# New homes for block 1's transposed activations and for the inner operands of a two-block MLP kernel

## The chip, the core and the metric

The kernel runs on one core of a Trainium2 chip. The metric is the device time of one execution, in microseconds (us), lower is better; the median of three runs stands for a kernel. The core has a matrix engine (TensorE, PE in the profile), a vector engine (VectorE, DVE), an activation engine (ScalarE, ACT), GpSimd (POOL) and SyncE (SP), which here issues nearly all transfers. Each engine works through its own list of instructions in order, and waits at semaphores for the others.

## The reference, cut to what matters

```python
B, S, D, F = 1, 2048, 1024, 3584          # all inputs bfloat16

def reference(x, w1, b1, w2, b2):
    y = _layernorm(x, axis=-1)            # over D, no scale, no shift
    h = _gelu(jnp.einsum("bsd,df->bsf", y, w1) + b1)    # tanh form
    return jnp.einsum("bsf,fd->bsd", h, w2) + b2
```

## The kernel before

The 2048 rows are worked on in two blocks of 1024 (`s` = 0 and 1). Both matrix products of a block use Strassen's scheme in Winograd's form: an operand is cut into quarters (11, 12, 21, 22), sums of quarters (S1 to S4 on one side, T1 to T4 on the other) are made on VectorE, and seven products (numbers 1 to 7) take the place of eight.

- The first product has 7 chunks of w1 per block (`NC` = 7), loaded into a ring of 3 slots. The chunks of both blocks are counted through: 0 to 6 in block 0, 7 to 13 in block 1; chunk `n` lies in slot `n % 3`.
- The second product runs its seven products in the order 5, 1, 2, 6, 7, 3, 4. Products 1 to 4 are cut once more into seven ("inner" products, `INNER`), whose operand sums need room: four X operands in the tile of the T sums of w1 (`t1_sb`), four Y operands of 7 x 256 = 1792 elements in the w1 ring. Inner product 4 has other places for them.
- `yw_sb` is shared. During the first product it holds the transposed activations: A11, A12, A21, A22 and the sums S1 to S4, in seven slots of 2048 elements (A21 and S3 share one). During the second product its quarter "C", the first 7168 elements (3.5 slots), holds the w2 operand of product 2.

Block 1 is prepared while block 0's second product runs: rows are loaded, normalized on ScalarE (`ln_act2`), transposed by DMA into `yw_sb` (`dma_T`), summed on VectorE (`y_sums`), and the first w1 chunks are loaded.

The order of the instructions on each engine isn't written by hand. Every operation is handed to a planner with its dependencies, a modelled cost and a priority; the planner simulates the engines, picks at each moment the most urgent operation among those that could start, and thereby fixes each engine's list. A changed dependency can therefore change the order on several engines.

```python
        YN = KH * HT                                    # 4 * 512 = 2048
        yop = {n: yw16[:, k * YN:(k + 1) * YN].rearrange("p (k n) -> p k n", n=HT)
               for k, n in enumerate(("A11", "A12", "A22", "S3", "S1", "S2", "S4"))}
        yop["A21"] = yop["S3"]
...
        w2q = {"A": w2a_sb[:, 0], "B": w2a_sb[:, 1], "C": quarter(yw_sb, 0), "D": quarter(yw_sb, 1)}
...
        def load_w1(s, c, prio, gate=(), eng="SP"):
            n = s * NC + c
            deps = [*w1_use.get(n - N_W1, ()), *gate]   # N_W1 = 3
            w1_ld[(s, c)] = [dma(w1_sb[:, n % N_W1, ...], ...) for j in range(2)]   # two halves of 512 KB
...
        def dma_T(s, i, prio, gate):                    # tile i of 8: 128 rows; halves k of D
            for k in range(2):
                res.append(add("SP", 1.4, lambda e, k=k: e.dma_start_transpose(
                    dst_y(i, k), x16[:, i, k * HT:(k + 1) * HT]), (y_ok[(s, i)], *gate[k]), ...))
        # dst_y: tiles 0 to 3 go to A11 (k = 0) and A12 (k = 1), tiles 4 to 7 to A21 and A22; TH = 4
...
        def y_sums(s, prio, gate=(), war=()):           # each sum in two instructions
            S1 = tt("S1", "A21", "A22", ALU.add, ())
            S2 = tt("S2", "S1", "A11", ALU.subtract, (S1,))
            S3 = tt("S3", "A11", "A21", ALU.subtract, (S1,))
            S4 = tt("S4", "A12", "S2", ALU.subtract, (S2,))
...
        def mm2_block(s, W):
            ...
            X0 = halves(t1_sb ...)
            Y0 = halves(w1_16 ...)                      # elements 0 to 7167 of the ring's 3 * 4096
            n = s * NC + NC - 1
            ...                                         # products 5, 1, 2, 6, 7
            B[2] = load_w2(s, "C", "B21", W["C"], base2[s])       # W["C"]: all matmuls of the first product
            ...
            sub3 = inner(3, S4, B[3], X0, Y0, ...)
            for m in range(n - 2, n + 1):
                w1_use[m] = w1_use[m] + done(3)         # the slots are released by inner product 3
            ...
            inner(4, A[22], B[4], ...)
            return {"A": done(3), "B": done(4), "C": done(2), "ring": ring, "w1": [(), (), ()]}
...
            if s + 1 < NSB:
                for c in range(N_W1):
                    load_w1(s + 1, c, base2[s] + 40 + c, wf["w1"][c])
                for i in range(NT):                     # 8 tiles
                    load_x(s + 1, i, [*x_gate[i]], base2[s] - 4 + i)
                    ln_act2(s + 1, i, base2[s] + 10 + 5 * i, wf["ring"])
                    dma_T(s + 1, i, base2[s] + 30 + 3 * i, (wf["C"], wf["C"]))
                y_sums(s + 1, base1[s + 1] - 14, wf["C"])
```

`w1_use[m]` are the instructions that read chunk `m`, so that the load into its slot three chunks later waits for them. `done(p)` are the matmuls and operand sums of product `p`. `last` (not in this cut) are the matmuls of the block's first product.

Of the kernel before, what the change touches and what calls it, by code (L numbers as in the profile page):

```python
# [26 lines left out]
N_W1 = 3  # L27
# [57 lines left out]
class Planner:  # L85
# [8 lines left out]
    def add(self, *a, **k):  # L94
        o = Op(*a, **k)
        self.ops.append(o)
        return o
# [139 lines left out]
def bass_standalone__mixer_channel_mlp__prompt_kernel(  # L237
# [19 lines left out]
    TH = HT // P  # L257
# [4 lines left out]
    with ExitStack() as es:  # L262
# [28 lines left out]
        w1_16 = w1_sb[:, :, :, :].bitcast(FP16)  # L291
# [6 lines left out]
        def quarter(t, k):  # L298
# [4 lines left out]
        tq = nc.dram_tensor("w2_sums", [4, P, NU, HT], FP16, kind="Internal").ap()  # L303
        YN = KH * HT
        yop = {n: yw16[:, k * YN:(k + 1) * YN].rearrange("p (k n) -> p k n", n=HT)
               for k, n in enumerate(("A11", "A12", "A22", "S3", "S1", "S2", "S4"))}
        yop["A21"] = yop["S3"]

        pl = Planner()
# [9 lines left out]
        base2 = [b + T_MM1 for b in base1]  # L319


        def dma(dst, src, deps, prio, name, sem, nbytes, eng="SP", late=0.0):
            return add(eng, 0.42 if eng == "SP" else 0.45, lambda e: e.dma_start(dst, src), deps, prio, name,
                       sem="d_" + sem, inc=16, nbytes=nbytes, late=late)
# [16 lines left out]
        def load_w1(s, c, prio, gate=(), eng="SP"):  # L341
            n = s * NC + c
            deps = [*w1_use.get(n - N_W1, ()), *gate]
            w1_ld[(s, c)] = [dma(w1_sb[:, n % N_W1, j * KH:(j + 1) * KH, :],
                                 w1v[:, j * KH:(j + 1) * KH, c * 4 * P:(c + 1) * 4 * P], deps, prio + 0.01 * j,
                                 f"w1_{s}_{c}_{j}", f"w1_{n % N_W1}_{j}", KH * P * 4 * P * 2, eng=eng) for j in range(2)]
# [114 lines left out]
        def dst_y(i, k):  # L461
            return yop[("A1" if i < TH else "A2") + "12"[k]][:, :, (i % TH) * P:(i % TH + 1) * P]
# [18 lines left out]
        def dma_T(s, i, prio, gate):  # L481
            res = []
            for k in range(2):
                res.append(add("SP", 1.4, lambda e, k=k: e.dma_start_transpose(  # L484
                    dst_y(i, k), x16[:, i, k * HT:(k + 1) * HT]), (y_ok[(s, i)], *gate[k]), prio + 0.05 * k,
                    f"yt{s}_{i}_{k}", sem=f"d_yt{i}{k}", inc=16, nbytes=P * HT * 2))
            x_free[(s, i)] = res
            y_in[(s, i)] = res
# [4 lines left out]
        def y_sums(s, prio, gate=(), war=()):  # L493
# [5 lines left out]
            def tt(n, x0, x1, op, dp):  # L499
                res = []  # L500
                deps = [o for x in (x0, x1) for o in src.get(x, ())]
                for g in range(2):
                    sl = slice(g * KP, (g + 1) * KP)
                    res.append(add("DVE", 0.64, lambda e, sl=sl: e.tensor_tensor(  # L504
                        out=yop[n][:, sl, :], in0=yop[x0][:, sl, :], in1=yop[x1][:, sl, :], op=op),
                        [*deps, *gate, *(war if n == "S3" else ())] + [d[g] for d in dp],
                        prio + {"S1": 0, "S2": 1, "S4": 2, "S3": 3}[n] + 0.1 * g, f"y{n}_{s}_{g}"))
                return res
# [5 lines that stand above are left out]
            opnd[s] = {n: [src[n]] * KH for n in ("A11", "A12", "A22")}  # L514
            for n, l in (("S1", S1), ("S2", S2), ("S3", S3), ("S4", S4)):
                opnd[s][n] = [[l[k // KP]] for k in range(KH)]
# [146 lines left out]
        KI = NU // 2  # L663
        HI = HT // 2
# [3 lines left out]
        def sums(dst, a, b, op, deps, prio, name, step=2):  # L668

            res = []  # L670
            n = len(a[1])
            cuts = step if isinstance(step, tuple) else tuple([step] * (n // step) + [n % step] * (n % step > 0))
            k0 = 0
            for g, w in enumerate(cuts):
                k1 = k0 + w
                dl = list(deps)
                for k in range(k0, k1):
                    dl += a[1][k] + b[1][k]
                o = add("DVE", cost2(w * dst.shape[-1]), lambda e, k0=k0, k1=k1: e.tensor_tensor(  # L679
                    out=dst[:, k0:k1, :], in0=a[0][:, k0:k1, :], in1=b[0][:, k0:k1, :], op=op),  # L680
                    list(dict.fromkeys(dl)), prio + 0.15 * k0, f"{name}_{g}")
                res += [[o]] * w
                k0 = k1
            return dst, res
# [4 lines left out]
        def uniq(*a):  # L689
            return list(dict.fromkeys(o for l in a for o in l))  # L690
# [55 lines left out]
        def mm2_block(s, W):  # L746
# [6 lines left out]
            A = {q: (h[q], [[h_ok[(s, q, u)]] for u in range(NU)]) for q in h}  # L753
            users = {p: [] for p in SEQ2}
            done = lambda p: users[p]
# [144 lines left out]
                return subs  # L900

            def halves(t):
                return [t[:, r * KI * HI:(r + 1) * KI * HI].rearrange("p (k n) -> p k n", n=HI) for r in range(4)]

            X0 = halves(t1_sb[:, :, :, :, :].rearrange("p a b k c -> p (a b k c)"))
            Y0 = halves(w1_16[:, :, :, :].rearrange("p a k c -> p (a k c)"))
            n = s * NC + NC - 1
            S1 = sums(h[21], A[21], A[22], ALU.add, (), pt[5] - 12, f"hS1_{s}")
            ring = uniq(*(w1_use[m] for m in range(n - 2, n + 1)), *(l for m in (n - 1, n) for l in t1_use[m].values()))
            war0 = {(c, r): ring + S1[1][-1] for c in "ST" for r in range(1, 8)}  # L910

            def war_of(subs):
                return {(c, r): [subs[r]] for c in "ST" for r in subs}

            B = dict(W)
# [6 lines left out]
            for t in range(TH):  # L922
# [5 lines left out]
            hb = [Holder(banks, seeded=True) for _ in range(TH)]  # L928
            g1, ok1, sub1 = inner(1, A[11], B[1], X0, Y0, war0, gate=(M5[2],), bias=(
                b2_sb[:, None, 0:HI].to_broadcast([P, 2, HI]), e0_sb[:, None, :].to_broadcast([P, 2, HI])))  # L930
# [3 lines left out]
            S2 = sums(h[11], S1, A[11], ALU.subtract, done(1), pt[2], f"hS2_{s}", step=(2, 4, 4, 4))  # L934
            S3 = sums(h[21], A[22], S2, ALU.subtract, done(5), pt[2] + 4, f"hS3_{s}", step=(4, 4, 4, 2))
# [3 lines left out]
            okw = {11: ok1[11], 12: sdb[1], 21: sdb[3], 22: sdb[3]}  # L939
            sub2 = inner(2, A[12], B[2], X0, Y0, war_of(sub1), O=(g1, okw), out=11)  # L940
            S4 = sums(h[12], A[12], S2, ALU.subtract, done(2), pt[6], f"hS4_{s}", step=(4, 4, 4, 2))
# [22 lines left out]
                               alloc=g3 if t == 0 else None, frees=(hb[t],)))  # L964

            sub3 = inner(3, S4, B[3], X0, Y0, war_of(sub2), O=(g12, {11: O12[1], 12: O12[1], 21: O12[3], 22: O12[3]}), out=12)
            for m in range(n - 2, n + 1):
                w1_use[m] = w1_use[m] + done(3)
            for m in (n - 1, n):
                for k in range(1, 5):  # L970
# [8 lines left out]
            hf = {11: done(4), 12: done(3), 21: done(4), 22: done(4) + flat(S3)}  # L979
            for q in h:  # L980
                h_war[(s + 1, q)] = hf[q]
            return {"A": done(3), "B": done(4), "C": done(2), "ring": ring, "w1": [(), (), ()]}

        tile_prio = [-100 + 2.3 * i for i in range(NT)]
        for i in range(NT):
# [19 lines left out]
        for s in range(NSB):  # L1005
            last = []
            for c in range(NC):
                n = s * NC + c
                t0 = base1[s] + c * 14 * SLOT
                if n:  # L1010
                    T = w1_sums(s, c, t0 - 2 * SLOT)
                    for v in range(2):
                        last += mm1_unit(s, c, v, T, t0 + v * SLOT)
                m = n + N_W1
                if m < (s + 1) * NC:
                    load_w1(s, m % NC, t0 + 14 * SLOT)
                if s == 0 and c == 1:
                    gate = (w1_use[0][-1],)
                    t11 = load_w2(0, "B", "B11", gate, t0 + 0.1)
                    t1q = w2_prep(t11[1][0][0], gate, t0 + 8, 8.5)  # L1020
            if s == 0:
                W = {5: t1q, 1: t11}
            else:
                W = {5: load_w2(s, "A", "T1", wfree["A"], base1[s] + 0.3 * T_MM1),
                     1: load_w2(s, "B", "B11", wfree["B"], base1[s] + 0.3 * T_MM1 + 0.1)}
            W["C"] = last
            wfree = wf = mm2_block(s, W)
            if s + 1 < NSB:
                for c in range(N_W1):
                    load_w1(s + 1, c, base2[s] + 40 + c, wf["w1"][c])  # L1030
                for i in range(NT):
                    load_x(s + 1, i, [*x_gate[i]], base2[s] - 4 + i)
                    ln_act2(s + 1, i, base2[s] + 10 + 5 * i, wf["ring"])
                    dma_T(s + 1, i, base2[s] + 30 + 3 * i, (wf["C"], wf["C"]))
                y_sums(s + 1, base1[s + 1] - 14, wf["C"])

        order = pl.place()
# [57 lines left out]
```

## Time and profile before

| what | value |
|---|---|
| time, median of 3 runs | 352.75 us (351.5 to 354.36) |
| span of the profiled run | 351.5 us |
| TensorE busy | 338.8 us, 96% |
| VectorE busy | 255.3 us, 73% |
| ScalarE busy | 183.6 us, 52% |
| DMA, mean of 16 engines | 179 GB/s |
| granted TensorE clock | 1.00 |

"Busy" is an average over the whole span. The stages, by TensorE's timeline: head and first chunk to about 30 us, block 0's first product to 100.2 us, its second product to about 175 us (with some of it up to 188 us), block 1's first product to 268.7 us, its second product to 347.9 us. In the lines of the profile, L604 are the matmuls of the first product, L792 those of the plain products of the second, L838 those of the inner products; L679 are the operand sums of the second product on VectorE, L504 those of the activations, L537 those of w1. `yw_sb<-x_sb` are the transposes, `w_sb<-in_w_dram` the loads of w1 (digits are dropped from names: `w_sb` is `w1_sb`, `t_sb` is `t1_sb`), `w2a_sb` two homes of w2 operands. SPq is the time that SyncE's queue took to issue transfers, not the transfers themselves. A bracket after a line is the idle time of the engine before it and what ended it.

### The profile page before, as it was taken

How to read it: one execution, taken by the hardware profiler on the slowest of the kernel's cores; microseconds unless marked ns; L12 is line 12 of the kernel's file. 1: busy time of each engine (PE TensorE's matmuls, PEld its weight loads, DVE VectorE, ACT ScalarE, POOL GpSimd, SP SyncE). 2: the span in 40 equal slices, each digit the busy share in tenths (PEclk: the TensorE clock that was granted, in tenths of full speed). 3: DMA queues.
4: the chain of work that ended last, by engine and by line, in shares of the span. 5: the costliest groups of instructions: out<-in, count | busy, mean ns of one | idle time of the engine just before them, and what ended most of it. 6: DMA issues, size and time to landing. Idle time of an engine off the chain costs nothing.

```text
span 351.5 us, 5462 instructions
## 1 busy us (share of the span) xinstructions
PE 338.8 (96%) x2179; PEld 202.6 (58%) x2179; DVE 255.3 (73%) x356; ACT 183.6 (52%) x303; POOL 23.5 (7%) x47
## 2 busy tenths in 40 slices
PE   4999999999999999999859999999999999999995
PEld 4987444444445876448735444444444488644885
DVE  5679988988575797969399665375338869896943
ACT  3674766766798888431113766767677234001110
POOL 2320000000004123600000000000000000000000
PEclk9999999999999999999999999999999999999999
DMA  7748999979863450798699730330002355019111
GB/s 233 247 91 279 354 341 342 300 270 300 277 202 85 186 211 21 140 385 129 154 370 339 259 97 24 119 119 2 0 0 87 123 212 210 32 48 400 62 62 60
DMA packets 54339, 63.01 MB, mean 179 GB/s; under 512 B 12970, under 2 KB 47786, under 8 KB 53418
## 3 DMA queue, kind: packets, MB, share of 16 engines
q1 hardware_dynamic: 54170, 62.54, 55.0%
q8 instruction: 17, 0.28, 0.3%
q10 hardware_dynamic: 144, 0.13, 0.1%
q14 instruction: 8, 0.07, 0.1%
HBM read 48.50 MB, written 11.53 MB: 171 GB/s over the span
## 4 chain that ended last, share of the span: by engine, by line
PE 85%; DVE 5%; DMA 4%; SPq 3%; issue 1%; ACT 1%; DVEq 0%
PE ps L604 44%; PE ps L838 20%; PE ps L792 15%; PE ps L562 5%; SPq L484 3%; DMA w2a_sb<-in_w_dram 2%; DVE h_sb L679 2%; DMA x_sb<-in_x_dram 1%; DVE o_sb L756 1%; DVE w_sb L679 1%; PE ps L468 1%; DVE yw_sb L504 1%; DMA yw_sb<-x_sb 1%; DVE sn_sb L756 0%; ACT h_sb L410 0%
## 5 line engine op out<-in xcount | busy, mean ns | idle before, releaser
L604 PE MATMUL ps<-yw_sb,t_sb 128*128 128x512 f16 x416 | 96.2, 379 | 0.0
L604 PE MATMUL ps<-yw_sb,w_sb 128*128 128x512 f16 x312 | 73.7, 379 | 1.8 <-DMA w_sb<-in_w_dram 1.8
L792 PE MATMUL ps<-w2a_sb,h_sb 128*128 128x512 f16 x336 | 73.8, 379 | 0.0
L604 PEld LDWEIGHTS ps<-yw_sb,t_sb 128*128 128x128 f16 x416 | 40.5, 98 | 48.8 <-ACT sn_sb L617 0.6
L622 DVE TENSOR_TENSOR sn_sb<-ps,sn_sb 128x512 f32<-128x512 f32 x54 | 36.6, 689 | 25.9 <-PE ps L604 25.8
L792 PEld LDWEIGHTS ps<-w2a_sb,h_sb 128*128 128x128 f16 x336 | 32.9, 98 | 38.4
L604 PEld LDWEIGHTS ps<-yw_sb,w_sb 128*128 128x128 bf16 x312 | 30.3, 98 | 38.3 <-DMA w_sb<-in_w_dram 2.1
L628 ACT ACTIVATE h_sb<-sn_sb,b_sb 128x512 f16<-128x512 f32 x54 | 38.6, 719 | 18.7 <-DVE sn_sb L622 16.3
L776 ACT COPY sn_sb<-ps 128x512 f32<-128x512 f32 x30 | 17.3, 581 | 46.9 <-DVE o_sb L756 34.8
L617 ACT COPY sn_sb<-ps 128x512 f32<-128x512 f32 x49 | 28.7, 586 | 23.1 <-PE ps L604 22.9
L679 DVE TENSOR_TENSOR h_sb<-h_sb 128x1024 f16<-128x1024 f16 (+2 forms) x42 | 38.6, 951 | 2.1 <-ACT h_sb L628 2.1
L628 ACT ACTIVATE h_sb<-ps,b_sb 128x512 f16<-128x512 f32 x50 | 34.1, 685 | 9.1 <-PE ps L604 8.2
L756 DVE TENSOR_TENSOR o_sb<-ps,sn_sb 128x512 bf16<-128x512 f32 x32 | 21.9, 688 | 13.5 <-PE ps L838 9.5
L838 PE MATMUL ps<-w_sb,t_sb 128*128 128x256 f16 x252 | 30.0, 273 | 0.0
L838 PEld LDWEIGHTS ps<-w_sb,t_sb 128*128 128x128 f16 x252 | 24.7, 98 | 3.1
L537 DVE TENSOR_TENSOR t_sb<-w_sb,t_sb 128x1024 f16<-128x1024 bf16 x26 | 17.9, 688 | 8.3 <-PE ps L604 7.9
L838 PE MATMUL ps<-w2a_sb,h_sb 128*128 128x256 bf16 (+1 forms) x182 | 21.8, 273 | 0.0
L537 DVE TENSOR_TENSOR t_sb<-w_sb 128x1024 f16<-128x1024 bf16 x26 | 17.8, 683 | 5.5 <-PE ps L604 4.1
L776 ACT COPY ps<-sn_sb 128x512 f32<-128x512 f32 x14 | 8.1, 588 | 24.4 <-PE ps L838 20.5
L679 DVE TENSOR_TENSOR t_sb<-h_sb 128x1792 f16<-128x1792 f16 x12 | 13.0, 1086 | 9.6 <-PE ps L838 9.5
L838 PEld LDWEIGHTS ps<-w2a_sb,h_sb 128*128 128x128 f16 x182 | 17.7, 98 | 3.2
L756 DVE TENSOR_TENSOR sn_sb<-ps,sn_sb 128x512 f32<-128x512 f32 x24 | 16.5, 686 | 4.2 <-PE ps L838 2.6
(82 smaller groups left out, 322.0 us busy)
## 6 DMA issues: line engine op xcount, KB each, us to landing
w_sb<-in_w_dram SPq DMA_DIRECT2D x28, 512.0 KB, 5.4
w2a_sb<-w_sums SPq DMA_DIRECT2D x5, 1792.0 KB, 7.5
w2a_sb<-in_w_dram SPq DMA_DIRECT2D x4, 1792.0 KB, 8.6
x_sb<-in_w_dram SPq DMA_DIRECT2D x21, 256.0 KB, 4.8
w_sums<-x_sb SPq DMA_DIRECT2D x21, 256.0 KB, 4.6
x_sb<-in_x_dram SPq DMA_DIRECT2D x15, 256.0 KB, 4.3
yw_sb<-in_w_dram SPq DMA_DIRECT2D x2, 1792.0 KB, 7.6
h_sb<-w_sums SPq DMA_DIRECT2D x2, 1792.0 KB, 11.5
```

The source lines that it names most:

```text
L484: res.append(add("SP", 1.4, lambda e, k=k: e.dma_start_transpose(dst_y(i, k), x16[:, i, k * HT:(k + 1) * HT]), (y_ok[(s, i)], *gate[k]), p ...
L537: return add("DVE", 0.65, lambda e: e.tensor_tensor(out=tv(k), in0=x0, in1=x1, op=ALU.subtract), [*deps, *war.get(k, ())], prio + 0.5 * k, ...
L562: fn = [(lambda e, b=b, hb=hold[f], f=f, k=k, t=t: e.matmul(ps[:, hb.k, t * P:(t + 1) * P], lhsT=lhs[:, k, f * P:(f + 1) * P], rhs=yop[f"A ...
L604: fn = [(lambda e, k=k: e.matmul(ps[:, hold[p].k, :], lhsT=lhs[:, k, :], rhs=yop[yo][:, k, :], start=(first and k == 0), stop=(k == KH - 1 ...
L617: return e.copy(out=dst, in_=src) if o_.eng == "ACT" else e.tensor_copy(dst, src)
L622: return add("DVE", 0.69, lambda e: e.tensor_tensor(out=sn_sb[:, hold_s.k, :], in0=ps[:, hold[p].k, :], in1=sn_sb[:, hold_s.k, :], op=ALU. ...
L628: r = h_ok[(s, q, u)] = add("ACT", 0.70, lambda e: e.activation(out=h[q][:, u, :], in_=src(), func=ACT.Gelu_apprx_tanh, bias=b1_sb[:, f:f ...
L679: o = add("DVE", cost2(w * dst.shape[-1]), lambda e, k0=k0, k1=k1: e.tensor_tensor(out=dst[:, k0:k1, :], in0=a[0][:, k0:k1, :], in1=b[0][: ...
L756: plus = lambda e, out, x, y: e.tensor_tensor(out=out, in0=x, in1=y, op=ALU.add)
L776: return act(lambda e: e.copy(out=out(), in_=src()), deps, at, name, **k)
L792: fn = [(lambda e, k=k, t=t: e.matmul(ps[:, banks_[t].k, :], lhsT=a[0][:, k, t * P:(t + 1) * P], rhs=b[0][:, k, :], start=(first and k == ...
L838: fn = [(lambda e, k=k, j=j: e.matmul(ps[:, bank[r].k, j * HI:(j + 1) * HI], lhsT=x[0][:, k, j * P:(j + 1) * P], rhs=y[0][:, k, :], start= ...
```

## The change

The change gives some data another place, so that transfers needn't wait for the data that lay there. The arithmetic is the same. It has three parts:

1. The order of the seven slots in `yw_sb` is turned: S1, S2, S4 take the first three, A11, A12, A22 the last three; A21 (with S3) stays in the fourth. The transposes into A11, A12 and A22 now wait for `last`, the end of block 0's first product; those into A21 (first half of tiles 4 to 7) also wait for product 2.
2. The four Y operands of the inner products are cut two and two from the ring slots of the chunks `n - 2` and `n`, and only these two slots wait for inner product 3. The slot of chunk `n - 1` is left to the next block's loads.
3. The empty gates `"w1": [(), (), ()]` of the loads are dropped, which alters nothing.

```diff
-               for k, n in enumerate(("A11", "A12", "A22", "S3", "S1", "S2", "S4"))}
+               for k, n in enumerate(("S1", "S2", "S4", "S3", "A11", "A12", "A22"))}
         yop["A21"] = yop["S3"]
...
-                return [t[:, r * KI * HI:(r + 1) * KI * HI].rearrange("p (k n) -> p k n", n=HI) for r in range(4)]
+                return [t[:, r * KI * HI:(r + 1) * KI * HI].rearrange("p (k n) -> p k n", n=HI)
+                        for r in range(t.shape[1] // (KI * HI))]
 
             X0 = halves(t1_sb[:, :, :, :, :].rearrange("p a b k c -> p (a b k c)"))
-            Y0 = halves(w1_16[:, :, :, :].rearrange("p a k c -> p (a k c)"))
             n = s * NC + NC - 1
+            Y0 = [y for m in (n - 2, n) for y in halves(w1_16[:, m % N_W1].rearrange("p k c -> p (k c)"))[:2]]
...
-            for m in range(n - 2, n + 1):
+            for m in (n - 2, n):
                 w1_use[m] = w1_use[m] + done(3)
...
-            return {"A": done(3), "B": done(4), "C": done(2), "ring": ring, "w1": [(), (), ()]}
+            return {"A": done(3), "B": done(4), "C": done(2), "ring": ring}
...
-                    load_w1(s + 1, c, base2[s] + 40 + c, wf["w1"][c])
+                    load_w1(s + 1, c, base2[s] + 40 + c)
...
-                    dma_T(s + 1, i, base2[s] + 30 + 3 * i, (wf["C"], wf["C"]))
+                    dma_T(s + 1, i, base2[s] + 30 + 3 * i, ((*last, *(wf["C"] if i >= TH else ())), last))
```

## The prediction, made before the changed kernel ran

> **What bounds the kernel now.** I read the page first. Part 1 gives TensorE (PE) 338.8 us of a 351.5 us span, part 2 a full granted clock in every slice, and the chain of waits is 85% PE. So a change of homes can only return time in which PE stands still. The waits of PE are the next view: engine, line, what it waited for, total us, times, longest.
>
> ```profile
> PE ps L838 <- DVE h_sb L679: 2.7, 1, 2.7
> PE ps L468 <- DVE x_sb L401: 2.5, 1, 2.5
> PE ps L604 <- DMA w_sb<-in_w_dram: 1.8, 1, 1.8
> PE ps L562 <- ACT yw_sb L475: 1.1, 1, 1.1
> PE ps L373 <- POOL ones L348: 1.0, 1, 1.0
> ```
>
> L468, L562 and L373 are the head of the kernel, before 9 us, which the diff doesn't touch. The other two are both at the seam between the two blocks. The timeline of PE (start us, busy us, then the idle time before it) places them:
>
> ```profile
> 173.14 1.69 PE L838 MATMUL ps<-h_sb 128*128 128x256 f16 x14
> 176.67 2.76 PE L604 MATMUL ps<-yw_sb,w_sb 128*128 128x512 f16 x12 [1.84 <-DMA w_sb<-in_w_dram]
> 182.12 1.69 PE L838 MATMUL ps<-h_sb 128*128 128x256 f16 x14 [2.69 <-DVE h_sb L679]
> ```
>
> PE idles 1.84 us for block 1's first w1 chunk and 2.69 us for an operand sum of block 0's last product: 4.53 us in all. After 182 us the PE timeline shows no other idle time to its end at 347.93 us, and a tail of 3.6 us follows. **The ceiling of this change is therefore 4.5 us, 1.3%.**
>
> Why are the two late? First the queue of SyncE (SP), which issues nearly all transfers, in order:
>
> ```profile
> 139.97 5.97 SPq L484 DMA_TRANSPOSE yw_sb<-x_sb  x4
> 146.60 0.47 SPq L323 DMA_DIRECT2D w2a_sb<-in_w_dram  x1
> 148.11 19.66 SPq L484 DMA_TRANSPOSE yw_sb<-x_sb  x10
> 168.44 2.51 SPq L484 DMA_TRANSPOSE yw_sb<-x_sb  x2
> 172.65 4.28 SPq L323 DMA_DIRECT2D w_sb<-in_w_dram  x6
> ```
>
> The 16 transposes of block 1's activations can't begin before product 2 of block 0 has read its w2 operand (at 139.9 us), because their destination lies over it. They then hold the queue for 5.97 + 19.66 + 2.51 = 28.1 us, although the usual issue takes 1.27 us (16 x 1.27 = 20.3 us). The w1 loads, whose buffer is released by inner product 3 (its last matmuls run 167.03 to 168.72 us), stand behind the last transposes and three stores: issued at 172.65, 3.9 us after they could have been.
>
> Then VectorE (DVE), in order of time:
>
> ```profile
> 172.27 2.50 DVE L504 TENSOR_TENSOR yw_sb<-yw_sb 128x1024 f16<-128x1024 f16 x4 [5.74 <-DMA yw_sb<-x_sb]
> 175.28 2.49 DVE L504 TENSOR_TENSOR yw_sb<-yw_sb 128x1024 f16<-128x1024 f16 x4
> 178.29 1.08 DVE L679 TENSOR_TENSOR h_sb<-h_sb 128x1792 f16<-128x1792 f16 x1
> 180.89 1.08 DVE L679 TENSOR_TENSOR h_sb<-h_sb 128x1792 f16<-128x1792 f16 x1
> ```
>
> DVE stands idle 5.74 us, blocked on the last transpose, then makes eight sums of block 1's activations, and only then the operand sums S3 and S4 of inner product 4. The second of them ends at 181.97 us: that is PE's 2.69 us wait. Both waits of PE thus go back to the late transposes.
>
> The sources of the transposes were ready long before. ScalarE's timeline has eight normalizations (L455); the first and the last:
>
> ```profile
> 108.35 1.24 ACT L455 ACTIVATE x_sb<-x_sb,st_sb,rstd_sb 128x1024 f16<-128x1024 bf16 x1 [0.28 <-POOL st_sb L452]
> 149.53 1.24 ACT L455 ACTIVATE x_sb<-x_sb,st_sb,rstd_sb 128x1024 f16<-128x1024 bf16 x1 [2.83 <-POOL st_sb L452]
> ```
>
> The eight end at 109.6, 115.8, 121.9, 128.8, 135.5, 139.3, 145.3 and 150.8 us.
>
> **What the Trainium skill says.** "DMA: Bandwidth & Descriptors", section "Anatomy of one DMA — SWDGE (gpsimd) path", says that the wait for a semaphore is made on the issuing sequencer, before dispatch; the transfers themselves wait for none. So one gated transfer delays every later one of its queue, which is what the SP timeline shows (w1 3.9 us late). "Advanced Engine Details and Errata", section "X-Bar Transpose (TRN2)", calls transposes as fast as other transfers, at 350 to 400 GB/s. This trace doesn't agree: 128 KB (128 x 512 x 2 bytes) each 1.27 us is 103 GB/s, and between 164 and 170 us, where transposes lead, the windows view shows 103 GB/s at a DMA share of 0.63. Here transposes are dear, and when they run matters. "PSUM — Partial Sum Buffer", section "Engine vs sequencer instructions", says that VectorE's queue is strictly first in, first out; the idle 5.74 us with ready sums behind it agrees.
>
> **The change, part by part.**
>
> *Part 1, the transposes.* Quarter "C" of the shared tile holds the w2 operand of product 2 and is 3.5 slots of 2048 elements long. A11, A12 and A22 move from slots 0, 1, 2 to 4, 5, 6, which no w2 operand of block 0 uses; A21 stays in slot 3, half in C. The gate becomes the end of block 0's first stage (about 100.2 us) for 12 of the 16 transposes; the four of A21 (first half of tiles 4 to 7) keep product 2. No instruction is added or removed.
> By the normalization times above, ten of the twelve (tiles 0 to 3, and the second half of 4 and 5) can be issued between 109.6 and about 140.5 us: 10 x 1.27 = 12.7 us of a queue that has only two issues between 112 and 139 us. Six are left after 139.9 us: 6 x 1.27 = 7.6 us. The last two wait for the normalization at 150.8, so are issued by about 153.3 us. Landing takes 2.6 us at the median and 11.3 at worst; the w2 loads issued at 146.60 and 147.12 land at 154.6 and about 158.6 (11.5 us), and the last transposes share the DMA engines with them. I put their landing at 156 to 161 us, against 172.1: 11 to 16 us earlier.
> The eight activation sums cost 5.0 us of DVE (two groups of four at 0.62 us pitch). They fit the idle 5.74 us (166.53 to 172.27), or come earlier among inner product 3's sums. S3 and S4, now behind them, move up by about 5.7 us: S3 from 179.3 to 173.6, S4 from 181.97 to 176.3. PE reaches a use for them at 174.67 at the earliest, when it also has matmuls of block 1 to do. **The 2.69 us should go, or nearly.**
>
> *Part 2, the SP queue.* With the transposes gone, the first w1 chunk's loads can be issued at about 168.8 instead of 172.65. The first half took 172.65 to 176.67 = 4.0 us to land; 168.8 + 4.0 = 172.8, before PE runs dry at 174.67 us. **The 1.84 us should go too.** This is the gain of part 1's freed queue, not of the ring.
>
> *Part 3, the ring slot.* The words of the change say the first w1 chunk of block 1. The indices say otherwise: n = 6 in block 0, so the inner operands now take chunks 4 and 6, slots 1 and 0 (4 mod 3, 6 mod 3). Block 1's chunks are 7, 8, 9, in slots 1, 2, 0. The slot given free is number 2, of the second chunk, 8. Before, the four operands of 1792 elements ended at 7168 of 12288 and slot 2 (from 8192) was never written; only the dependency held chunk 8. So this part lets 2 x 512 KB be loaded soon after 90 to 100 us and takes them out of the crowd at 173 us (DMA share 0.97 in 173 to 180 us). Chunk 7, for which PE waits, keeps its wait for inner product 3. I give this part 0 to 0.5 us of PE time, inside the 1.84.
>
> The sum: ceiling 2.69 + 1.84 = 4.53; I expect about five sixths of it, 3.75 us. 352.75 - 3.75 = **349.0 us**.
>
> **Rivals.**
> *A new wait of DVE.* All queues are fixed in order by a planner with modelled times. If it places the activation sums at, say, 158 us and the last transposes land at 161, DVE blocks there, ahead of inner product 3 and 4's sums. For it: in the kernel before, the plan misjudged the same arrival by 5.74 us, and DVE is busy 8.4 of 10 us between 158 and 168. Against it: PE has waited nowhere between 140 and 173 us, so there is some slack. PE would stand 1 to 3 us: 350 to 352 us.
> *The w1 load stays the bound.* Its release (168.72 us) isn't moved; if stores or transposes still stand ahead of it, or landing takes the 5.4 us median of its row, only the 2.69 us come back: about 350.3 us.
> *Earlier traffic collides.* Ten transposes and 1 MB more lie between 90 and 140 us and could delay the w2 sums loaded for products 6 and 7. Against it: the DMA share is 0.37 in 112 to 140 us; the load at 112.48 takes 7.5 us and is needed at 129.10, some 9 us later. I see no loss.
> *All hidden anyway:* against it stand two named waits of PE that both end in these transfers.
>
> **Range and chances.** Full removal gives 348.2, one gap kept 350 to 351, a new wait 350 to 352; the three runs of before spread from 351.5 to 354.36, so I widen by about a microsecond: 347.6 to 352.0. Faster by over 2% would need 7.1 us, more than PE idles at the seam: 3%. Slower by over 2% would need a new wait of 7 us: 2%.
>
> **What would show it.** Right: PE's waits for w_sb and h_sb at the seam are gone or under 0.5 us each; ten transposes before 141 us; the activation sums end before 172 us; two w_sb loads near 90 to 105 us; the first w1 load after 168 us issued by 169.5. Wrong: a DVE idle time with a transpose as its end, followed by a PE wait for t_sb, w_sb or h_sb between 155 and 185 us; transposes that take 2 us or more each in the queue beside other loads; w1 still issued after 171 us. The prediction fails as a whole if the planner's new order costs PE time outside the seam.

## Result and profile after

The changed kernel takes 347.36 us (median of 4 runs, 347.11 to 347.71), against 352.47 us (4 runs) beside it: a ratio of 0.9849, 95% interval 0.9806 to 0.9892. Repeated with more runs it took 347.79 us (6 runs) against 352.01 us (13 runs), ratio 0.9865 (0.9828 to 0.9903). The prediction was 349.0 us with a range of 347.6 to 352.0: the direction and the place were right, the gain of 3.75 us was put too small. The first time lies 0.24 us under that range, the repeated one inside it.

The waits of TensorE (PE) in the changed kernel, all of them (engine, line, what was waited for, total us, times, longest):

```profile
PE ps L468 <- DVE x_sb L401: 2.6, 1, 2.6
PE ps L373 <- POOL ones L348: 1.0, 1, 1.0
PE ps L562 <- ACT yw_sb L475: 0.6, 1, 0.6
```

Only the head of the kernel is left. The seam, in PE's timeline, has no idle time in brackets any more:

```profile
172.44 1.69 PE L838 MATMUL ps<-h_sb 128*128 128x256 f16 x14
173.97 3.62 PE L604 MATMUL ps<-yw_sb,w_sb 128*128 128x512 f16 x16
177.42 1.69 PE L838 MATMUL ps<-h_sb 128*128 128x256 f16 x14
```

SyncE's queue in the changed kernel, its transposes and the w1 loads of block 1:

```profile
85.88 0.93 SPq L323 DMA_DIRECT2D w_sb<-in_w_dram  x2
...
108.92 2.51 SPq L484 DMA_TRANSPOSE yw_sb<-x_sb  x2
...
115.10 7.29 SPq L484 DMA_TRANSPOSE yw_sb<-x_sb  x3
...
123.05 12.95 SPq L484 DMA_TRANSPOSE yw_sb<-x_sb  x4
...
138.85 1.21 SPq L484 DMA_TRANSPOSE yw_sb<-x_sb  x1
...
140.73 6.44 SPq L484 DMA_TRANSPOSE yw_sb<-x_sb  x4
...
150.10 5.21 SPq L484 DMA_TRANSPOSE yw_sb<-x_sb  x2
...
169.58 2.04 SPq L323 DMA_DIRECT2D w_sb<-in_w_dram  x4
```

Ten transposes are issued by 140 us, and the last two from 150.10 us in place of 168.44. (A merged line's time includes the waits between its members: in the stretch of 12.95 us the queue mostly waits for ScalarE, whose normalizations start there at 126.81 and 133.54 us.) VectorE (DVE), the activation sums and then S3 and S4 of inner product 4:

```profile
162.55 1.28 DVE L504 TENSOR_TENSOR yw_sb<-yw_sb 128x1024 f16<-128x1024 f16 x2
...
165.35 1.29 DVE L504 TENSOR_TENSOR yw_sb<-yw_sb 128x1024 f16<-128x1024 f16 x2
...
169.76 2.49 DVE L504 TENSOR_TENSOR yw_sb<-yw_sb 128x1024 f16<-128x1024 f16 x4
...
172.76 1.08 DVE L679 TENSOR_TENSOR h_sb<-h_sb 128x1792 f16<-128x1792 f16 x1
...
175.36 1.09 DVE L679 TENSOR_TENSOR h_sb<-h_sb 128x1792 f16<-128x1792 f16 x1
```

No bracket with a transpose: VectorE doesn't wait for one at the seam (its one such wait, 1.32 us, is in the head, before 26 us). S4 is done at 176.4 us, 1 us before PE reads it at 177.42.

### The profile page after: what moved, and what is told of

Its sections match the earlier page's. It is cut to its first block, busy times and chain, and to the rows that moved or that the text cites. A ratio compares the mean times of both kernels' runs of the same rounds, so it can differ in the third digit from the quotient of the medians.

```text
span 346.0 us, 5462 instructions
## 1 busy us (share of the span) xinstructions
PE 338.3 (98%) x2179; PEld 202.3 (58%) x2179; DVE 255.3 (74%) x356; ACT 183.4 (53%) x303; POOL 23.5 (7%) x47
## 4 chain that ended last, share of the span: by engine, by line
PE 97%; DMA 1%; ACT 1%; SPq 0%; DVE 0%; issue 0%
PE ps L604 45%; PE ps L838 25%; PE ps L792 21%; PE ps L562 5%; DMA x_sb<-in_x_dram 1%; PE ps L468 1%; ACT h_sb L410 0%; SPq L323 0%; DVE o_sb L756 0%; ACT yw_sb L475 0%; ACT mv_sb L412 0%; PE ps L379 0%
## 5 line engine op out<-in xcount | busy, mean ns | idle before, releaser
L792 PE MATMUL ps<-w2a_sb,h_sb 128*128 128x512 f16 x336 | 73.8, 379 | 0.0
L792 PEld LDWEIGHTS ps<-w2a_sb,h_sb 128*128 128x128 f16 x336 | 32.9, 98 | 38.4
```

The lines of the kernel that those rows point to most:

```text
L792: fn = [(lambda e, k=k, t=t: e.matmul(ps[:, banks_[t].k, :], lhsT=a[0][:, k, t * P:(t + 1) * P], rhs=b[0][:, k, :], start=(first and k == ...
```

## Experiments

The head varies from run to run by more than the smaller effects here. So beside each time stands what the profile of the run gives for the rest: the span less the start of block 0's second product (the first `L792` line of PE's timeline).

| kernel | time, us | ratio to before (95%) | head, us | rest, us |
|---|---|---|---|---|
| before | 352.47 | | 100.20 | 251.30 |
| changed | 347.36 | 0.9849 (0.9806 to 0.9892) | 99.50 | 246.50 |
| changed, repeated | 347.79 | 0.9865 (0.9828 to 0.9903) | 99.68 | 246.52 |
| homes only | 347.92 | 0.9870 (0.9844 to 0.9897) | 99.47 | 246.43 |
| ring only | 352.15 | 0.9984 (0.9965 to 1.0004) | 99.77 | 250.73 |
| half the homes | 346.81 | 0.9851 (0.9816 to 0.9885) | 99.92 | 246.38 |
| true first slot | 347.87 | 0.9859 (0.9835 to 0.9882) | 100.44 | 246.46 |
| sums late, nothing moved | 348.66 | 0.9884 (0.9855 to 0.9914) | 100.95 | 247.05 |
| w1 on ScalarE's queue, nothing moved | 357.90 | 1.0147 (1.0119 to 1.0175) | 98.89 | 257.01 |
| both of these, nothing moved | 349.11 | 0.9915 (0.9881 to 0.9949) | 98.90 | 249.00 |
| w1 on ScalarE's queue after the transposes | 352.16 | 0.9982 (0.9968 to 0.9997) | 98.26 | 251.04 |
| changed, longer warm-up | 346.44 | 0.9837 (0.9801 to 0.9873) | 98.22 | 246.48 |

The seam is worth 251.30 - 246.50 = 4.80 us. Times of different rows were in part taken on different chips; the ratios are to runs of before on the same chip.

**The two parts apart.** Homes only: the slot order and the transposes' gates of the change, with `Y0` and the release of all three w1 slots as before.

```diff
-               for k, n in enumerate(("A11", "A12", "A22", "S3", "S1", "S2", "S4"))}
+               for k, n in enumerate(("S1", "S2", "S4", "S3", "A11", "A12", "A22"))}
-                    dma_T(s + 1, i, ..., (wf["C"], wf["C"]))
+                    dma_T(s + 1, i, ..., ((*last, *(wf["C"] if i >= TH else ())), last))
```

> The change without its ring part: the Y operands and the release of all three w1 slots stay as before. My theory (the transposes hold SyncE's and VectorE's queues, the ring is a side matter): 347.4 to 348.0 us, no wait of TensorE at the seam, first w1 load of block 1 issued at about 169, six loads there. Rival (the early load of the second chunk is what relieves the seam): about 350 us, with a wait of TensorE for w1 of 1 us or more left.

Ring only is the rest of the change, with these two lines as before.

> The ring part alone, the transposes as before. My theory: 352.0 to 352.7 us, nothing gained, because the first chunk keeps its release and its place behind the transposes; both waits stay (1.8 and 2.7 us) though the second chunk's load is issued near 86 us. Rival (the ring is worth half the gain): about 350 us.

Homes only gives the whole seam (246.43 us). Ring only moves the second chunk's load ahead, and both waits stay in PE's list:

```profile
PE ps L838 <- DVE h_sb L679: 2.4, 1, 2.4
PE ps L604 <- DMA w_sb<-in_w_dram: 1.6, 1, 1.6
```

Against 2.7 and 1.8 in before that is 0.5 us less, and the rest is 0.57 us shorter, but the interval of the times includes 1. By its one profile the ring part alone is worth about 0.6 us, which the times don't confirm; beside the homes it shows nothing (246.50 against 246.43).

**Which queue?** The prediction named two blocked queues, SyncE's (w1 late) and VectorE's (S4 late). Each was relieved alone, in the kernel before. For SyncE's, the first chunk's loads were issued by ScalarE:

```diff
-                    load_w1(s + 1, c, base2[s] + 40 + c, wf["w1"][c])
+                    load_w1(s + 1, c, base2[s] + 40 + c, wf["w1"][c], eng="ACT" if c == 0 else "SP")
```

> The kernel before, with nothing moved; only the two loads of block 1's first w1 chunk are issued from ScalarE's queue, so that they don't stand behind transposes and stores. They should be issued by about 169 us and land before 174.7. Theory A (the two waits are separate and each is worth its length): 1.8 us gained, 350.6 us. Theory B (VectorE's late sum alone sets the time, and the wait for w1 only takes up a part of the same idle time): 352.0 to 352.8 us, the wait for w_sb gone and the wait for the sum in h_sb grown from 2.7 to about 4.5 us.

Neither theory: it lost 5.2 us. The loads were issued at 167.50 us, as meant, and PE's wait for w1 is gone; but it then waits twice for VectorE. The first line is of DVE's timeline, the next two are of PE's:

```profile
174.39 2.50 DVE L504 TENSOR_TENSOR yw_sb<-yw_sb 128x1024 f16<-128x1024 f16 x4 [9.16 <-DMA yw_sb<-x_sb]
```

```profile
177.64 1.02 PE L604 MATMUL ps<-yw_sb,w_sb 128*128 128x512 f16 x4 [2.38 <-DVE o_sb L756]
184.24 3.14 PE L838 MATMUL ps<-h_sb 128*128 128x256 f16 x14 [5.58 <-DVE h_sb L679]
```

VectorE's wait for the last transpose grew from 5.74 to 9.16 us: the slowest transpose issued at 165 to 172 us took 6.3 us to land, in before 4.2. The lines are before's and then this run's:

```profile
DMA to landing us min/median/max: 2.4/3.1/4.2
DMA to landing us min/median/max: 2.5/4.6/6.3
```

With 1 MB of w1 in flight beside it, the transfer that mattered more was delayed; S4 came later still, and PE waited 5.58 us for it. And then PE itself was slow: 14 matmuls took 3.14 us, where they take 1.69. The windows view (stretch, length, PE busy, ..., granted clock, DMA share, GB/s) has the reason:

```profile
175.28:178.69 3.41, 1.02 (x4) 0.32 (x4) 3.41 (x7) 0.00 (x0) 0.00 (x0) 1.00 1.09 349
...
176.00:179.00 3.00, 1.02 (x4) 0.32 (x4) 3.00 (x6) 0.00 (x0) 0.00 (x0) 0.95 1.08 356
...
178.80:179.00 0.20, 0.00 (x0) 0.00 (x0) 0.20 (x1) 0.00 (x0) 0.00 (x0) 0.50 1.10 348
...
179.00:184.00 5.00, 0.00 (x0) 0.00 (x0) 5.00 (x7) 0.57 (x1) 0.00 (x0) 0.50 1.09 412
184.00:187.00 3.00, 2.76 (x14) 1.93 (x15) 2.30 (x4) 0.57 (x1) 0.00 (x0) 0.50 0.72 288
187.00:190.00 3.00, 3.00 (x18) 2.11 (x17) 1.51 (x3) 0.00 (x0) 0.00 (x0) 0.68 0.28 89
```

The granted clock is at half from 178.8 us, when the 5.58 us of idle time (from 178.66) had only begun, and it stays there until about 189 us. So, by this view, the length of that idle time can't be the cause. In the 3.41 us before the fall PE had idled 2.38 us and worked 1.02 us. The Trainium skill, "TensorE: Matmul & The Clock Gate", section "Part 1: The HAM clock gate", puts the slow clock after an idle window of about 3.4 us; here the fall came without 3.4 us of unbroken idle time. In before, with 2.76 us of matmuls between idle times of 1.84 and 2.69 us, the clock stayed full; where the limit lies isn't shown. The loss adds up: PE idles 2.38 + 5.58 = 7.96 us in place of 4.53, and the two slow groups of 14 matmuls (3.14 and 2.56 us in place of 1.69) cost another 2.3 us, together about the 5.7 us by which the rest is longer.

To see whether the collision or ScalarE's queue was to blame, the same loads were also made to wait for the last two transposes to land (the lines of the loads stand behind those of the transposes for it):

```diff
+                    load_w1(s + 1, c, base2[s] + 40 + c, x_free[(s + 1, NT - 1)] if c == 0 else (),
+                            eng="ACT" if c == 0 else "SP")
```

> As the run with the first w1 chunk on ScalarE's queue, with one condition more: the two loads also wait until the last two transposes have landed (about 172 us). Theory (the slowdown of that run came from w1 transfers in flight beside the last transposes, which put off VectorE's activation sums and with them S3 and S4): the slowdown is gone, 351.5 to 353 us, waits of TensorE about as before (w1 1 to 2 us, h_sb 2 to 3.5 us, 4.5 us together), no sunk clock at the seam. Rival (issuing from ScalarE's queue is itself what costs, by holding up its copies): 356 us or more again.

The slowdown is gone (352.16 us, rest 251.04): VectorE's wait for the last transpose is 5.47 us again and the slowest landing 3.8 us. The waits that are left are not the expected ones, though. None is for w1; the loads, held back, now hold up ScalarE's copies behind them, and PE waits for these. The first two lines are ScalarE's, the others PE's:

```profile
170.05 0.95 ACTq L323 DMA_DIRECT2D w_sb<-in_w_dram  x2
171.09 0.59 ACT L776 COPY ps<-sn_sb 128x512 f32<-128x512 f32 x1 [12.34 <-DVE yw_sb L504]
```

```profile
172.25 1.70 PE L838 MATMUL ps<-w2a_sb,h_sb 128*128 128x256 f16 x14 [2.41 <-ACT sn_sb L776]
179.92 1.69 PE L838 MATMUL ps<-h_sb 128*128 128x256 f16 x14 [1.84 <-DVE h_sb L679]
```

So ScalarE's queue can cost PE time when a gated load stands in it, 2.41 us here. It did not in the run before this one: there the same copy ran at 169.03 us, after an idle time that PE ended. What cost 5.2 us there was the collision, and the slow clock that came with it.

For VectorE's queue, only the priority number of the activation sums was changed:

```diff
-                y_sums(s + 1, base1[s + 1] - 14, wf["C"])
+                y_sums(s + 1, base1[s + 1] - 4, wf["C"])
```

> The kernel before, with nothing moved; only the priority number of block 1's activation sums is raised by 10, so that the planner places them behind the operand sums S3, S4, T3, T4 of inner product 4. VectorE should no longer idle 5.7 us for the last transpose with ready work behind. Theory A (two separate waits): 2.7 us gained, 349.8 us, the wait for w1 kept. Theory B (VectorE's order alone sets the time): 4 to 5 us gained, 347.5 to 348.5 us, with transposes and w1 loads as late as before. Rival C (the late activation sums only move the wait to the first matmuls that read S1): 350 us or more, with a wait of TensorE for yw_sb or t_sb.

One number, no home moved, and 4.25 of the seam's 4.80 us are back (rest 247.05). Transposes and w1 loads are as late as before (SyncE's queue):

```profile
168.99 2.51 SPq L484 DMA_TRANSPOSE yw_sb<-x_sb  x2
171.54 2.05 SPq L785 DMA_DIRECT2D out_dram<-o_sb  x4
173.63 5.58 SPq L323 DMA_DIRECT2D w_sb<-in_w_dram  x6
```

but S3 and S4 fill the time in which VectorE had stood idle, and the first activation sum follows (DVE's timeline):

```profile
167.20 1.08 DVE L679 TENSOR_TENSOR h_sb<-h_sb 128x1792 f16<-128x1792 f16 x1
...
170.40 1.08 DVE L679 TENSOR_TENSOR h_sb<-h_sb 128x1792 f16<-128x1792 f16 x1
...
173.17 0.68 DVE L504 TENSOR_TENSOR yw_sb<-yw_sb 128x1024 f16<-128x1024 f16 x1
```

PE then does all of inner product 4 until 180.00 us and doesn't need w1 earlier:

```profile
178.47 1.69 PE L838 MATMUL ps<-w2a_sb,h_sb 128*128 128x256 f16 x14
180.00 1.89 PE L604 MATMUL ps<-yw_sb,w_sb 128*128 128x512 f16 x8
```

This is a new order of PE's list too: in before, and in the changed kernel, matmuls of block 1 stand ahead of those that read S4. So the edit moved two lists, and what VectorE's order gives with PE's list as before was not run. What is shown is that the gain needs neither new homes nor earlier transfers, as theory B has it (348.66 us is just above its range). What is left is 0.5 us, a new wait of PE for `sn_sb`.

Both edits together, nothing moved:

> The kernel before with the higher priority number of the activation sums and, with it, the first w1 chunk of block 1 issued from ScalarE's queue. Nothing is moved to another home. Theory (what hurt when w1 went to ScalarE's queue was that the earlier w1 transfer delayed the last transposes, with S3 and S4 behind them in VectorE's list): with S3 and S4 ahead of the activation sums the same delay costs nothing or under 1 us, 348 to 349.5 us, about as with the priority alone. Rival (the earlier w1 transfer itself costs TensorE time, whatever VectorE's order): 351 us or more, with a wait of 2 us or more.

349.11 us is in the theory's range, but the wait of 2.44 us is the rival's sign. The collision is there again (the slowest transpose took 6.8 us to land), VectorE still met it, now with a PSUM addition behind it instead of S4, and PE waited for that. The lines are of DVE's and of PE's timeline:

```profile
174.62 0.69 DVE L504 TENSOR_TENSOR yw_sb<-yw_sb 128x1024 f16<-128x1024 f16 x1 [3.42 <-DMA yw_sb<-x_sb]
```

```profile
175.97 1.70 PE L838 MATMUL ps<-w2a_sb,h_sb 128*128 128x256 f16 x14 [2.44 <-DVE sn_sb L756]
```

By these profiles the earlier w1 transfer costs 2 us (249.00 against 247.05) although nothing waits for w1; the times don't separate the two kernels (their ratios' intervals overlap, and the eight runs here spread from 347.97 to 353.40).

**How much of the change is needed.** Only the eight transposes of tiles 0 to 3 let go early:

```diff
-                    dma_T(..., ((*last, *(wf["C"] if i >= TH else ())), last))
+                    dma_T(..., ((*last, *(wf["C"] if i >= TH else ())), (*last, *(wf["C"] if i >= TH else ()))))
```

> The changed kernel, but only the eight transposes of tiles 0 to 3 are let go at the end of the first product; all eight of tiles 4 to 7 wait for product 2. If the gain comes from the last transpose landing before VectorE reaches the activation sums, and eight early ones are enough for that: 347.4 to 348.2 us, as the whole change. If each transpose left behind costs its 1.27 us on the queue: two more behind 140 us, 2.5 us of queue, 349 to 350 us with a wait of TensorE of 1 to 2 us.

346.81 us, rest 246.38: the whole gain. Eight early transposes are enough; the two more that the change lets go before 140 us add nothing.

The slot that the words of the change name, `Y0` in the slots of chunks `n - 1` and `n`:

```diff
-            Y0 = [y for m in (n - 2, n) for y in halves(...)[:2]]
+            Y0 = [y for m in (n - 1, n) for y in halves(...)[:2]]
-            for m in (n - 2, n):
+            for m in (n - 1, n):
```

> The changed kernel with the Y operands in the slots of chunks n - 1 and n in place of n - 2 and n, so that the slot left free is truly that of block 1's first w1 chunk. Theory (TensorE no longer waits for w1 at the seam, so an earlier load has nothing to give): the same as the changed kernel, 347.3 to 348.0 us, with two w1 loads issued before 90 us and the lists of TensorE and VectorE unchanged. Rival (the seam still hides a bit of waiting for w1): 0.5 us or more faster.

No difference (rest 246.46), though two w1 loads now go out at 74.73 us: an earlier load of a chunk that nothing waits for.

**The head.** The changed kernel with a longer warm-up:

```diff
-N_WARM = 26
+N_WARM = 48
```

> The changed kernel with 48 in place of 26 of the dummy matmuls that open the kernel, so that TensorE is busy until about 6.4 us in place of 4.0 (0.11 us each by the trace) and idles less than 1 us before the first transposes of the head. Theory (the head differs from run to run because TensorE's granted clock sinks after idle time there, as the slice of 0.6 to 0.7 in one profile with a head 1.4 us longer hints): 0.2 to 0.8 us faster than the changed kernel, 346.8 to 347.5, and its runs nearer to each other. Rival (the head is set by the load and normalization of the first tile, at any clock): the same as the changed kernel.

346.44 us (346.24 to 347.04, 5 runs), on the same chip as the repeated changed kernel's 347.79 (346.46 to 348.06, 6 runs): faster by 1.35 us, more than was expected, and with runs nearer to each other. The opening of PE's timeline, first of the changed kernel repeated, then of this one:

```profile
1.04 2.95 PE L373 MATMUL ps<-ones 128*128 128x128 f16 x26 [1.04 <-POOL ones L348]
6.54 1.03 PE L468 MATMUL ps<-ident,x_sb 128*128 128x128 f16 x8 [2.54 <-DVE x_sb L401]
7.92 1.87 PE L562 MATMUL ps<-yw_sb,w_sb 128*128 128x128 f16 x16 [0.34 <-ACT yw_sb L475]
```

```profile
1.04 4.51 PE L373 MATMUL ps<-ones 128*128 128x128 f16 x48 [1.04 <-POOL ones L348]
6.29 0.62 PE L468 MATMUL ps<-ident,x_sb 128*128 128x128 f16 x8 [0.74 <-DVE x_sb L401]
7.66 1.07 PE L562 MATMUL ps<-yw_sb,w_sb 128*128 128x128 f16 x16 [0.75 <-DMA w_sb<-in_w_dram]
```

The same 16 matmuls take 1.87 us after the short warm-up and 1.07 after the long one: in the first kernel PE runs at about half speed there, and does so until almost 13 us (eight L468 matmuls take 1.06 us at 9.58 us, 0.61 us at 12.97). The head is 1.46 us shorter (98.22 against 99.68), the rest the same. The heads of the other kernels go with the same thing: the first L468 group back at full speed starts at 9.69 us with a head of 98.26 (w1 after the transposes), at 12.97 with 99.68 (changed, repeated), at 14.15 with 100.95 (sums late). Of the kernels run here this has the lowest time, though its interval overlaps that of the changed kernel.

## Why the prediction was wrong, point by point

- **What bounds the kernel: right.** The gain is idle time of PE at the seam, and nothing else: all kernels without waits there have a rest of 246.4 to 246.5 us.
- **The ceiling: too low by 0.27 us.** It was read as idle time, 1.84 + 2.69 = 4.53 us. The rest shrank by 4.80. The idle column counts from the end of a group of matmuls, but running groups overlap: 14 matmuls last 1.69 us, while the next group starts 1.53 us after their start. Each stop loses that overlap of 0.16 us too, and 2 x 0.16 = 0.32 us covers the difference.
- **The step that failed: "I expect about five sixths of it".** The sum took 3.75 of 4.53 us and held back 0.78 us with no working shown for it; its rivals name new waits, but no view had shown one. None came, and all of the seam, 4.80 us, came back. 352.75 - 4.80 = 347.95 would have been 0.6 us from the result. Of that 0.6, 0.28 is the other median of before (352.47, with a fourth run), and the other 0.3 is within what heads differ by (98.2 to 101.0 us over these runs). The range had the same fault: full removal gave 348.2, and the lower end of 347.6 is only 0.6 us under it, not the microsecond that the text says.
- **Part 1: right, nearly to its numbers.** Ten transposes before 141 us; the last one landed at 160.1 us (156 to 161 was expected); S3 and S4 were put at 173.6 and 176.3 us and ended at 173.8 and 176.4; the activation sums ended at 172.3, a little after the 172 that was named.
- **Part 2: right for this kernel, but not the only way, and by a thin margin.** The first w1 load left at 169.58 us (168.8 was expected, 169.5 named as the limit), took 4.0 us to land, so until 173.6, and PE reads it at 173.97. With the issue at 172.65 us as before, PE would have had to wait in this list (an estimate from these numbers; no run here tries it). But the 1.84 us can't be had by an earlier w1 alone: with that wait gone PE waited for VectorE or ScalarE instead (4.25 us in one run, 7.96 in the other), and the reordered kernel gets 4.25 us back with w1 as late as ever. Behind PE's waits in before stands VectorE, blocked on the last transpose ahead of S3 and S4.
- **Part 3: right.** The freed slot is the second chunk's (its loads leave at 85.88 us), and the part shows no gain beside the homes.
- **Rivals.** The new wait of VectorE didn't come, with 2.4 us to spare (the last transpose landed at 160.1 us, the first activation sum starts at 162.55). One sign of being wrong did come, a transpose that held the queue for 3.97 us (from 151.3 us), and cost nothing. "The w1 load stays the bound" didn't come either, with the 0.4 us named above to spare; that so little was enough is in part luck. "Earlier traffic collides" was wrong for the stage it named, but right as a mechanism in a stage it didn't: w1 beside the last transposes.

## What to carry to other kernels

When an in-order engine idles with ready work behind the instruction that waits, look first at its order: one priority number, which let the planner reorder VectorE and PE, was worth 4.25 us here, nearly as much as moving the homes. Two waits of the critical engine close together may hang on the same late work, and removing one can just uncover the next; undo them one at a time, and look at every engine's new list. A transfer that is brought forward must be asked what it then runs beside. And where a cause is traced and the views show no new wait, predict the whole of it, with the overlap that each stop loses.

## What the runs showed that I had not expected

- 1 MB of w1 loads beside the last transposes raised their slowest landing from 4.2 to 6.3 and 6.8 us, and through VectorE's order cost up to 5.2 us of the whole.
- The granted clock fell to half at about 178.7 us, after 3.41 us in which PE had worked only 1.02 us, and stayed there until about 189 us; 14 matmuls took 3.14 in place of 1.69 us.
- In the head, after a warm-up of 2.95 us and 2.54 us of idle time, matmuls ran at about half speed until almost 13 us, although the granted clock of that profile reads 1.00 there. In the profile of the sums placed late it reads 0.50 from 7.6 to 14 us, with the same 1.86 us for those 16 matmuls. Here the durations tell, not the clock row.
